# Retention and SwiGLU on one core: norms, token sums and weight sums dealt out as single operations, attention begun in a group's last unit

## The chip, the cores and the metric

The kernel runs on one NeuronCore of a Trainium2 chip. Five engines work beside each other, each with a queue of instructions that it takes strictly in order: TensorE (PE in the profile; its weight loads are PEld), VectorE (DVE), ScalarE (ACT), GpSimd (POOL) and SyncE (SP), which issues DMA transfers. An instruction that waits for a semaphore holds up everything behind it in its own queue. The metric is the device time of one execution in microseconds, here the median of repeated runs.

## The reference

Four sequences of 768 tokens with eight heads of 64 columns go through retention (a linear attention with decay, in blocks), and the result, 3072 tokens by 512 columns, through a gated MLP with 1536 hidden columns.

```python
for b in range(nb):                                  # blocks of a sequence
    intra = np.einsum('bhic,bhjc->bhij', qb, kb) * Dmask[None]
    intra = np.einsum('bhij,bhjd->bhid', intra, vb)
    inter = np.einsum('bhid,bhde->bhie', qb * lam_pow[None], kv_state)
    out[:, :, sl] = intra + inter
    kv_state = lam_block * kv_state + np.einsum('bhsd,bhse->bhde', kb_dec, vb)
...
xn = x / np.sqrt(np.mean(x * x, axis=-1, keepdims=True) + 1e-6) * rms_g
g, val = xn @ w_gate, xn @ w_val
out = (g / (1 + np.exp(-g)) * val) @ w_out
```

## The kernel before, in words

The 3072 tokens are six groups `m` of 512, and the hidden columns are twelve slices `f` of 128. A unit is one slice for one group: gate and value products, SiLU times value, and the product with 128 rows of `w_out`, which adds to four PSUM accumulators. To keep single-precision accuracy each operand is split into a high and a low half-precision part, and a product takes three passes (high by high, low by high, high by low).

The units run in this order (variable `u`): 0 to 5 are slices 0 to 5 of group 0, in a written-out opening that also loads and splits the weights; 6 to 17 are group 1; 18 to 23 are slices 6 to 11 of group 0; 24 to 35 are group 2, and 36 to 47, 48 to 59 and 60 to 71 are groups 3, 4 and 5. Up to unit 23 a unit (`unit`) has 24 gate and value matmuls 512 wide. From unit 24 on (`unit_of_sums`) a unit takes seven products of half that size instead of eight, a Winograd-like scheme over the two halves of the gate and value weights and of the token columns. It needs sums of weight blocks (`weight_sums`) and sums of token blocks (`Norm.sums`), each again split into a high and a low part.

Three kinds of work run beside the units:

- **Attention.** A group has four head pairs (`Pair`). A pair takes two units: in the first (`new`) scores (L479), decays of k (ACT, L489), of the scores (DVE, L495) and of q (POOL, L499), and in the second (`done`) state sums, states (DVE, L523), the mix (L539, L550), the copy of the output (ACT, L571), its squares (ACT, L582) and their sum (L588). In groups 2 to 4 the pairs of the next group stand in units 0 to 7: `new` in even units, `done` in odd ones.
- **The norm of the next group** (`Norm`) stands in units 8 to 11 of a group: squares split (step 8), their column sums on TensorE, a seed (L658, L662), three Newton steps of three DVE operations each (`refine`, L669 to L671; one in step 8, two in step 9), then `parts(0)` in step 10 and `parts(1)` in step 11: two scalings (L679), four sums (L695 to L698), casts to the high parts (ACT, L684, L701) and the low parts (L687, L705). For group 2 this stands in units 21 to 23.
- **Weights.** `halve_o` turns a slice of `w_out` into half-precision parts (ACT, ACT, DVE, POOL: L263, L264, L265, L268), two slices in each of units 18 to 23. `weight_sums(f)` does for slice f two POOL additions that make whole weights (`r`, L805), four DVE sums (`ws`, L808 to L811), three ACT casts (L815 to L817) and three POOL subtractions (L818 to L820). It is issued whole at the end of units 18 to 23 (slices 0 to 5) and 26 to 31 (slices 6 to 11).

The order is that of the code: `tc.manual_schedule` keeps every engine's instructions in the order in which the Python code issues them. In a product unit the DVE order that matters is: `sum` into `val` (left), the low part of the unit before (`hh`, L940), attention's decay or states, `sum` into `sg` (right), `sum` into `val` (right), then `mul_sums` (L909). On ACT: `keep` (L897), the high part of the unit before (L933), two more `keep`, then `silu_half(1)`, `silu_half(0)` (L904). TensorE's product banks are one double tile (`pp`) in one unit and two single tiles (`pa`, `pb`) in the next; before, `pp` is that of odd `u`.

In units up to 23 the DVE multiplication that ends a unit is L922, in later units L909; both are used below as the tick of a unit.

## Time and profile before

| | us |
|---|---|
| median of 3 runs (767.11 to 783.88) | 767.44 |
| the profiled execution's own time | 771.88 |
| its span, first to last instruction | 769.9 |
| TensorE busy | 675.0 |
| VectorE busy | 420.5 |
| ScalarE busy | 329.9 |
| GpSimd busy | 161.0 |
| mean granted TensorE clock | 0.949 of full |

A row of a group view gives engine, line of the kernel, operation, tiles as out<-in, their shapes, and how often; a timeline row begins with start and duration in us; a row of the chain of waits gives start, duration and what the end of the run depended on then. A row of a stretch gives its bounds, its length, each engine's busy time with the instructions in brackets, the granted clock, the DMA share and GB/s.

### The profile page before, as it was taken

The page shows a single profiled execution, that of the slowest core. Times are in us where ns is not written, and L with a number is a line of the kernel's source. Part 1 is how long each engine was busy: PE and PEld are TensorE (multiplying, and loading weights), DVE is VectorE, ACT ScalarE, POOL GpSimd, SP SyncE. Part 2 cuts the span into 40 slices and gives each one's busy share as a digit, 9 for nine tenths or more (in the row PEclk, how much of TensorE's full clock was granted, in tenths as well). Part 3 has the DMA queues.
Part 4 walks back from the last instruction along what each step waited for, and adds up shares of the span by engine and source line. Part 5 has one row for each costly group of instructions (what it writes and reads, how often), then busy time and mean ns, then how long its engine had stood idle before and what let it go on. Part 6 is the DMA issues. An engine that isn't in the chain of part 4 may idle for free.

```text
span 769.9 us, 12275 instructions
## 1 busy us (share of the span) xinstructions
PE 675.0 (88%) x5007; PEld 450.4 (58%) x5007; DVE 420.5 (55%) x793; ACT 329.9 (43%) x674; POOL 161.0 (21%) x150
## 2 busy tenths in 40 slices
PE   9999999999987718887977799997899997799997
PEld 8656655556543305655645577765577765566664
DVE  7898667874446754435464543365444456443333
ACT  4786457762354342433333343333343433343332
POOL 3101200111367343354422101102101101100000
PEclk9999999999988957989999999998899999899999
DMA  8966224311300001111100031110031000010001
GB/s 326 331 229 209 110 85 162 137 55 35 131 1 1 0 1 55 55 55 55 55 2 1 1 110 56 55 56 1 0 111 55 2 1 1 0 55 1 1 1 55
DMA packets 14311, 51.12 MB, mean 66 GB/s; under 512 B 1712, under 2 KB 1968, under 8 KB 12848
## 3 DMA queue, kind: packets, MB, share of 16 engines
q1 hardware_dynamic: 13968, 49.69, 18.2%
q8 instruction: 39, 0.64, 0.3%
q10 hardware_dynamic: 288, 0.66, 0.3%
q14 instruction: 16, 0.13, 0.1%
HBM read 44.05 MB, written 6.29 MB: 65 GB/s over the span
## 4 chain that ended last, share of the span: by engine, by line
PE 69%; DVE 16%; ACT 8%; POOL 4%; issue 2%; DMA 1%; DVEq 0%; SPq 0%; ACTq 0%; POOLq 0%
PE pp L854 13%; PE pa L854 8%; PE acc L741 7%; PE pg L722 6%; PE pv L722 6%; PE acc L743 6%; PE acc L742 6%; PE pb L854 6%; PE pa L479 3%; PE po L539 3%; POOL r L805 2%; PE po L550 2%; DVE xn L679 1%; DVE sg L909 1%; DVE yt L670 1%
## 5 line engine op out<-in xcount | busy, mean ns | idle before, releaser
L742 PE MATMUL acc<-wo,hh 128*128 128x512 f16 (+1 forms) x288 | 113.3, 393 | 0.0
L743 PE MATMUL acc<-wo,hh 128*128 128x512 f16 (+1 forms) x288 | 113.1, 393 | 0.0
L854 PEld LDWEIGHTS <-wo 128*128 128x128 f16 x576 | 57.7, 103 | 66.3 <-issue 44.7
L741 PE MATMUL acc<-wo,hh 128*128 128x512 f16 x216 | 85.6, 396 | 0.2 <-DVE hh L940 0.2
L854 PEld LDWEIGHTS <-wg 128*128 128x128 f16 x576 | 56.4, 98 | 47.4 <-issue 26.5
L854 PEld LDWEIGHTS <-wv 128*128 128x128 f16 x576 | 58.0, 101 | 28.3 <-issue 19.7
L722 PE MATMUL pg<-x,wg 128*128 128x512 f16 x288 | 67.8, 380 | 3.3 <-ACT sg L915 3.0
L897 ACT COPY tx<-pp 128x256 f32<-128x256 f32 x72 | 26.7, 371 | 102.5 <-PE pp L854 102.5
L722 PE MATMUL pv<-x,wv 128*128 128x512 f16 x288 | 66.8, 379 | 0.0
L897 ACT COPY tx<-pa 128x256 f32<-128x256 f32 x72 | 26.8, 372 | 87.9 <-PE pa L854 87.6
L933 ACT CAST hh<-sg 128x512 f16<-128x512 f32 (+1 forms) x72 | 44.5, 618 | 39.4 <-DVE sg L922 19.3
L854 PE MATMUL pp<-tx,wo 128*128 128x256 f16 x288 | 42.5, 287 | 21.5 <-DVE vals L900 21.5
L854 PE MATMUL pp<-x,wg 128*128 128x256 f16 x288 | 40.5, 278 | 22.6 <-ACT sg L904 17.8
L900 DVE TENSOR_TENSOR vals<-pp,tx 128x256 f32<-128x256 f32 x48 | 20.3, 424 | 61.2 <-PE pp L854 50.1
L499 POOL TENSOR_TENSOR qkv<-qkv,pw 128x512 f32<-128x512 f32 x22 | 28.5, 1298 | 113.9 <-PE pa L479 108.4
L722 PEld LDWEIGHTS <-wg 128*128 128x128 f16 x288 | 26.4, 98 | 36.8 <-issue 7.8
L940 DVE TENSOR_TENSOR hh<-sg,hh 128x512 f16<-128x512 f32 x54 | 41.5, 768 | 11.1 <-ACT hh L933 8.7
L722 PEld LDWEIGHTS <-wv 128*128 128x128 f16 x288 | 27.6, 98 | 33.3 <-issue 1.1
L900 DVE TENSOR_TENSOR vals<-pb,tx 128x256 f32<-128x256 f32 x48 | 20.3, 424 | 46.7 <-PE pb L854 38.4
L909 DVE SCALAR_TENSOR_TENSOR sg<-vals,cv,sg 128x512 f32<-128x512 f32 x48 | 39.0, 812 | 9.0 <-ACT sg L904 5.9
L854 PE MATMUL pa<-x,wv 128*128 128x256 f16 x144 | 21.8, 290 | 19.1 <-ACT sg L915 9.9
L743 PEld LDWEIGHTS <-hh 128*128 128x128 f16 x216 | 21.8, 101 | 27.7 <-issue 3.8
(179 smaller groups left out, 1255.7 us busy)
## 6 DMA issues: line engine op xcount, KB each, us to landing
qkv<-in_qkv_dram SPq DMA_DIRECT2D x47, 512.0 KB, 5.1
raw_gv<-in_weights_dram SPq DMA_DIRECT2D x11, 1024.0 KB, 6.0
raw_o<-in_weights_dram SPq DMA_DIRECT2D x12, 512.0 KB, 4.0
out_dram<-o SPq DMA_DIRECT2D x23, 256.0 KB, 2.1
partial<-in_weights_dram SPq DMA_DIRECT2D x2, 512.0 KB, 11.6
qkv<-in_qkv_dram ACTq DMA_DIRECT2D x1, 512.0 KB, 4.3
out_dram<-o SPq DMA_DIRECT2D x1, 128.0 KB, 2.1
out_dram<-o ACTq DMA_DIRECT2D x1, 128.0 KB, 1.9
```

The lines of the kernel that those rows point to most:

```text
L479: nc.tensor.matmul(self.pa[:, j, c, :], self.kT[r, c, :], self.qT[r, c, :], start=True, stop=True,)
L499: eng.tensor_mul(self.qT, self.qT, pw[:, p : p + 1, :].broadcast_to([P, GC, P]))
L722: nc.tensor.matmul(ps, w[:, kk, :], x[:, kk, :], start=i == kk == 0, stop=i == 2 and kk == NK - 1,)
L741: nc.tensor.matmul(acc, hl[:, ts_], oh, start=first, stop=False)
L742: nc.tensor.matmul(acc, hh[:, ts_], ol, start=False, stop=False)
L743: nc.tensor.matmul(acc, hh[:, ts_], oh, start=False, stop=last)
L854: nc.tensor.matmul(ps, w(ow, k), x(ox, k), start=first and i == k == 0, stop=i == 2 and k == 1, skip_group_check=True,)
L897: nc.scalar.copy(self.kept[:, i], self.pa)
L900: nc.vector.tensor_add(out, self.pb, self.kept[:, i])
L909: nc.vector.scalar_tensor_tensor(self.sg, self.val, cv[:, self.f : self.f + 1], self.sg, ALU.mult, ALU.mult)
L933: nc.scalar.copy(self.hh, self.sg)
L940: nc.vector.tensor_sub(self.hl, self.sg, hh)
```

## The change

1. `weight_sums` becomes a class with four steps. `whole` (POOL) is issued at the end of the unit before, `sums` (DVE) within the unit, `high` (ACT) and `low` (POOL) after it. The slices go to units 18, 19, 20 and then 24 to 32, one each. `halve_o` goes to units 18, 19, 20 with three slices each, and to 24, 25, 26 with one each; units 21 to 23 keep only the norm.
2. The norm's operations in units 8 to 11 become a list of single tasks with assumed costs; after `add(5)` and before `add(4)` each unit takes from it what fits a given room (1.4 to 2.9). The ACT casts have a list of their own. Row sums and seed stand in step 7 instead of 8; what is left when the group ends is issued then.
3. Attention of the next group begins one unit earlier: the first pair's `new` stands in unit 11 of the group before (in unit 23 for group 3), so `new` has odd and `done` even units. The banks swap with it: `pp` is now that of even `u`.
4. `val` and `kept` are one buffer each instead of two that alternate; scaled tokens take the tiles of the seed.

```diff
-    def weight_sums(f, rest):
...
+    class WeightSums:
...
+        def whole(self, u):
...
+            for i, w in enumerate((wv, wg)):
+                nc.gpsimd.tensor_add(self.r[:, i], w[:, f, 0], w[:, f, 1])
...
+        def high(self):
+            for to, t in self.places():
+                nc.scalar.copy(to[:, 0], t)
...
+        def low(self, eng=nc.gpsimd):
+            for to, t in self.places():
+                eng.tensor_sub(to[:, 1], t, to[:, 0])
...
-            self.val = vals[u % 2]
-            self.kept = copies[u % 2]
+            self.kept = spare[0]
+            self.val = spare[1].rearrange("p a g -> p (a g)")
...
-    HALVE = {18: [6, 7], 19: [8, 9], 20: [10, 11], 21: [0, 1], 22: [2, 3], 23: [4, 5]}
+    HALVE = {18: [6, 7, 8], 19: [9, 10, 11], 20: [0, 1, 2], 24: [3], 25: [4], 26: [5]}
+    SUMS = {u: WeightSums(f) for f, u in enumerate([18, 19, 20, *range(24, 33)])}
...
+        def run(self, room):
+            while self.todo and self.todo[0][0] <= room + 0.05:
+                cost, fn, args = self.todo.pop(0)
+                room -= cost
+                fn(*args)
...
+        casts.run(1.5)
         h.add(5, b, True)
...
-        if norm and step == 9:
-            norm.refine()
-            norm.refine()
+        if u in SUMS:
+            SUMS[u].sums(u)
+        tasks.run(1.6 if attention or u in SUMS else 2.9)
         h.add(7, a)
         h.keep(0)
         h.sum(h.sg[:, right], 0)
         h.silu_half(1, h.sg[:, right])
+        if u in SUMS:
+            SUMS[u].high()
+            SUMS[u].low()
...
-        if norm and step == 10:
-            norm.parts(0, (nc.gpsimd, nc.gpsimd, nc.gpsimd))
-        if norm and step == 11:
-            norm.parts(1, (nc.vector, nc.vector, nc.gpsimd))
+        for i in HALVE.get(u, []):
+            halve_o(i)
+        if norm:
+            norm.row_sums()
+            norm.seed()
+        else:
+            tasks.run(1.4)
         h.add(4, a)
...
+            if u == 2 * NF - 1:
+                new = Pair(3, 0)
...
+            following = m + 2 if f == NF - 1 else m + 1
+            if f % 2 and p < NP and following < NG:
+                new = Pair(following, p)
+            if f % 2 == 0:
+                done = pair
```

Where it moves instructions, at three places that the prediction uses.

**DVE, units 8 and 9 of group 3** (tiles: `hy`, `yt` the norm of group 4, `pss` its sums, `pb_3_8` and `pp_3_9` the product banks, `sg` the SiLU input). Before:

```order
L900 TENSOR_TENSOR sg_3_8_4541<-pb_3_8_4540,tx_0_2466 128x256
L658 TENSOR_SCALAR hy_4_4599<-pss_4_4596 128x512
L662 TENSOR_SCALAR hy_4_4599<-hy_4_4599 128x512
L669 TENSOR_TENSOR yt_4_4600<-hy_4_4599 128x512
L670 TENSOR_TENSOR yt_4_4600<-yt_4_4600,hy_4_4599 128x512
L671 SCALAR_TENSOR_TENSOR hy_4_4599<-yt_4_4600,hy_4_4599 128x512
L900 TENSOR_TENSOR vals_2638<-pb_3_8_4540,tx_0_2466 128x256
L909 SCALAR_TENSOR_TENSOR sg_3_8_4541<-vals_2638,cv_138,sg_3_8_4541 128x512
```

Now, in unit 8:

```order
L976 TENSOR_TENSOR hh_3_7_4557<-sg_3_7_4465,hh_3_7_4557 128x512
L671 TENSOR_TENSOR yt_4_4524<-hy_4_4523 128x512
L673 TENSOR_TENSOR yt_4_4524<-yt_4_4524,hy_4_4523 128x512
L675 SCALAR_TENSOR_TENSOR hy_4_4523<-yt_4_4524,hy_4_4523 128x512
L671 TENSOR_TENSOR yt_4_4524<-hy_4_4523 128x512
L936 TENSOR_TENSOR sg_3_8_4543<-pp_3_8_4542,tx_0_2458 128x256
L673 TENSOR_TENSOR yt_4_4524<-yt_4_4524,hy_4_4523 128x512
L675 SCALAR_TENSOR_TENSOR hy_4_4523<-yt_4_4524,hy_4_4523 128x512
L936 TENSOR_TENSOR tx_1_2459<-pp_3_8_4542,tx_0_2458 128x256
```

Five operations of the norm stood in one block behind the SiLU's sum; now four stand ahead of it and two behind.

**POOL, units 18 and 19** (group 0, slices 6 and 7; `rest` and `wo16` of the halvings, `r` the whole weights, `ws` the weight sums, `sq_2` the squares of attention, `qkv` its q). Before:

```order
L268 TENSOR_TENSOR wo16_6_2093<-rest_6_2094 128x512
L268 TENSOR_TENSOR wo16_7_2099<-rest_7_2100 128x512
L588 TENSOR_TENSOR sq_2_1994<-sq_2_1994,sq_2_1_2123 128x512
L805 TENSOR_TENSOR r_0_2153<-wv_131 128x512
L805 TENSOR_TENSOR r_0_2153<-wg_130 128x512
L818 TENSOR_TENSOR wo16_6_2093<-ws_0_2156,wo16_6_2093 128x512
L819 TENSOR_TENSOR col_133<-ws_0_2156,col_133 128x256
L820 TENSOR_TENSOR wg_130<-ws_0_2156,wg_130 128x256
```

Now, in the same units:

```order
L268 TENSOR_TENSOR wo16_6_2101<-rest_6_2102 128x512
L268 TENSOR_TENSOR wo16_7_2107<-rest_7_2108 128x512
L268 TENSOR_TENSOR wo16_8_2113<-rest_8_2114 128x512
L857 TENSOR_TENSOR wo16_6_2101<-ws_0_2028,wo16_6_2101 128x512
L857 TENSOR_TENSOR col_133<-ws_0_2028,col_133 128x256
L857 TENSOR_TENSOR wg_130<-ws_0_2028,wg_130 128x256
L588 TENSOR_TENSOR sq_2_1994<-sq_2_1994,sq_2_1_2143 128x512
L829 TENSOR_TENSOR r_1_2173<-wv_131 128x512
L829 TENSOR_TENSOR r_1_2173<-wg_130 128x512
```

The subtractions of slice 0 now stand ahead of the squares, the whole weights behind them are those of the next slice (`r_1`), and three halvings instead of two stand in front.

**ACT, a unit of group 2 with `done` attention and weight sums** (before unit 27, now unit 26; `sg` the two SiLU halves, `x_3` and `sq_3` the output of attention and its squares). Before:

```order
L904 ACTIVATE sg_2_3_2924<-sg_2_3_2924,cg_136 128x256
L571 COPY x_3_2800<-po_3_1_2961 128x512
L904 ACTIVATE sg_2_3_2924<-pp_2_3_2923,cg_136 128x256
L582 ACTIVATE sq_3_1_3012<-po_3_1_2961 128x512
L815 CAST wo16_1_2418<-ws_7_3029 128x512
L816 CAST partial_96<-ws_7_3029 128x256
L817 CAST wg_130<-ws_7_3029 128x256
```

Now:

```order
L940 ACTIVATE sg_2_2_2816<-sg_2_2_2816,cg_136 128x256
L852 CAST wo16_11_2249<-ws_5_2873 128x512
L852 CAST col_133<-ws_5_2873 128x256
L852 CAST wg_130<-ws_5_2873 128x256
L571 COPY x_3_2681<-po_3_1_2850 128x512
L263 ACTIVATE wo16_5_2904<-wo_5_1046,ts_132 128x512
L264 ACTIVATE rest_5_2905<-wo_5_1046,ts_132 128x512
L940 ACTIVATE sg_2_2_2816<-pp_2_2_2815,cg_136 128x256
L582 ACTIVATE sq_3_1_2925<-po_3_1_2850 128x512
```

The three casts, and in units 24 to 26 two operations of a halving, now stand between the two SiLU halves instead of behind both.

More of the change, by code (lines that the diff above doesn't have):

```diff
@@ L1356, in unit @@
         elif norm:
-            norm.parts(step - NP - 2, (nc.vector, nc.vector, nc.gpsimd))
+            norm.parts(step - NP - 2)
         if before:
@@ L1392, in out @@
                 outs.out(*ts)
+        attention = new or done
         h.banks(u)
@@ L1407, in unit_of_sums @@
             new.decay_q()
-        elif done:
+        elif done and not begun:
             done.state_sums()
-        if not new:
+        else:
             out(0)
-        if norm and step == 8:
+        if norm:
             norm.split_squares()
```

198 lines of the change are left out of this document (125 added, 73 removed).

## The prediction

> **What bounds the kernel now.** The page first, then stretches of it, then the ticks of the units.
>
> ```profile
> span 769.9 us, 12275 instructions
> PE 675.0 (88%) x5007; PEld 450.4 (58%) x5007; DVE 420.5 (55%) x793; ACT 329.9 (43%) x674; POOL 161.0 (21%) x150
> ```
>
> TensorE is busy 88% of the span, so about 95 us can be won from its waits, and more if its busy time shrinks. Up to unit 18, at 191 us, the order is the same but for POOL's first whole weights, so I begin with the stretch behind them (bounds, length, busy time of PE, PEld, DVE, ACT, POOL; granted clock):
>
> ```profile
> 191.73:303.80 112.07, 76.77 (x451) 41.97 (x450) 61.40 (x104) 42.08 (x78) 55.53 (x50) 0.82 0.09 33
> ```
>
> Units 18 to 23 and the start of group 2 leave TensorE idle for 35 of 112 us, at a clock of 0.82. The ticks L909 (DVE, start and duration) measure the groups from there on:
>
> ```profile
> 303.77 0.75 DVE L909 SCALAR_TENSOR_TENSOR sg<-vals,cv,sg 128x512 f32<-128x512 f32 x1
> 320.80 0.75 DVE L909 SCALAR_TENSOR_TENSOR sg<-vals,cv,sg 128x512 f32<-128x512 f32 x1
> 384.57 0.75 DVE L909 SCALAR_TENSOR_TENSOR sg<-vals,cv,sg 128x512 f32<-128x512 f32 x1
> ...
> 440.78 0.75 DVE L909 SCALAR_TENSOR_TENSOR sg<-vals,cv,sg 128x512 f32<-128x512 f32 x1
> 558.69 0.75 DVE L909 SCALAR_TENSOR_TENSOR sg<-vals,cv,sg 128x512 f32<-128x512 f32 x1
> 577.22 0.75 DVE L909 SCALAR_TENSOR_TENSOR sg<-vals,cv,sg 128x512 f32<-128x512 f32 x1
> 675.11 0.75 DVE L909 SCALAR_TENSOR_TENSOR sg<-vals,cv,sg 128x512 f32<-128x512 f32 x1
> 683.44 0.75 DVE L909 SCALAR_TENSOR_TENSOR sg<-vals,cv,sg 128x512 f32<-128x512 f32 x1
> 690.61 0.75 DVE L909 SCALAR_TENSOR_TENSOR sg<-vals,cv,sg 128x512 f32<-128x512 f32 x1
> ```
>
> These are unit 0 of group 2, its units 2 and 7, unit 0 of groups 3 and 4, unit 2 of group 4, and units 0, 1, 2 of group 5. From unit 0 to unit 0, group 2 takes 137.0, group 3 117.9, group 4 116.4. Two plain units take 15.5 (8.33 and 7.17, the double bank `pp` being the slower), two units with a pair of attention 18.5 (558.69 to 577.22). Four pairs and four plain units would be 4 x 18.5 + 2 x 15.5 = 105. So 12 us a group are the norm's, and 20 more in group 2 the weight sums': its units 3 to 7 take 12.75 each (320.80 to 384.57).
>
> What such a stall is made of, for the weight sums of unit 18 and the start of the next units, in the chain of waits (start, duration, what):
>
> ```profile
> 202.54 0.71 ACT rest L264
> 203.25 0.47 ACT x L571
> ...
> 204.21 0.97 ACT o L748 x2
> ...
> 205.85 2.79 DMA out_dram<-o
> ...
> 208.77 2.27 POOL r L805 x2
> 211.06 0.43 DVE ws L808
> ...
> 212.31 0.47 ACT wo L815
> ...
> 213.54 0.81 ACT qkv L489 x2
> ...
> 214.96 0.75 DVE sg L922
> ...
> 218.26 0.67 DVE rest L265
> ...
> 228.88 0.76 DVE sg L922
> ...
> 231.01 0.70 DVE rest L265
> ```
>
> An output transfer frees a buffer, POOL makes the whole weights, DVE sums, ACT casts, and only behind the casts comes the next unit's SiLU, then its tick (L922) at 214.96. The halvings follow, then POOL again: one ring through four engines. And the norm, in units 8 to 11 of group 3:
>
> ```profile
> 511.09 0.70 DVE hy L658
> ...
> 512.27 0.70 DVE yt L669
> ...
> 529.23 1.32 DVE xn L679 x2
> ...
> 532.05 1.14 ACT x L684 x2
> 533.19 0.73 ACT tx L701
> ...
> 535.95 1.44 PE pp L854 x6
> ```
>
> Seed, Newton steps, scalings, sums and casts stand in the chain themselves, while TensorE waits; it comes back at 535.95 with 1.44 us for six matmuls.
>
> **Part 1: units 18 to 23.** More rows of its steps: the tick of unit 18, a unit's value product, the first product of unit 24 that isn't held, and POOL's operations.
>
> ```profile
> 197.41 0.75 DVE L922 SCALAR_TENSOR_TENSOR sg<-pv,cv,sg 128x512 f32<-128x512 f32 x1 [0.87 <-PE pv L722]
> ```
>
> ```profile
> 172.43 2.59 PE pv L722 x12
> ```
>
> ```profile
> 287.06 1.22 PE L854 MATMUL pa<-x,wv 128*128 128x256 f16 x5 [9.18 <-ACT x L684]
> ```
>
> ```profile
> 213.01 1.15 POOL L818 TENSOR_TENSOR wo<-ws,wo 128x512 f16<-128x512 f32 x1 [1.98 <-ACT wo L815]
> 215.38 1.27 POOL L499 TENSOR_TENSOR qkv<-qkv,pw 128x512 f32<-128x512 f32 x1
> ...
> 280.52 1.26 POOL L268 TENSOR_TENSOR wo<-rest 128x512 f16<-128x512 f32 x1 [1.77 <-DVE rest L265]
> 282.71 1.64 POOL L268 TENSOR_TENSOR wo<-rest 128x512 f16<-128x512 f32 x1 [0.93 <-DVE rest L265]
> ```
>
> Before: 197.41 to 287.06, 89.7. A slice's subtractions take 2.4 (213.01 to 215.38), its whole weights 2.3, its sums 1.7 (1.25 to 212.31, and a fourth), its casts 1.2 (to 213.54), a halving's addition 1.3. The tiles `ws` and `rest` share two buffers; since `ws` now lives through the halvings, these run on one, as at 280.52 and 282.71: 2.2 apart.
>
> - Unit 18, from its tick: first halving on DVE +3.5 (it was 3.3 from 214.96 to 218.26), the third 4.4 later, its copy on ACT 0.7: +8.6. Casts 1.2, output and squares 1.0, two output copies 1.0: +11.8. The buffer is free 3.6 later (205.18 to 208.77), whole weights and sums with their gaps 4.2: **19.6**. It was 17.6 (197.41 to 214.96).
> - Unit 19: the third halving's addition ends at +9.8 (3.3 + 4.4 + 0.8 + 1.3), then subtractions 2.4, squares 1.3, whole weights 2.3, sums 1.8: **17.6**.
> - Unit 20, without attention's decay and states: the halvings start at +2.1 (228.88 to 231.01); copy, casts, output and squares end at +9.4. Only then is the value bank free for unit 21, whose twelve matmuls take 2.6, or 5.2 at the half pace that follows a wait. TensorE has waited; I take 4.3: **13.7**.
> - Unit 21, norm alone: 2.1, seed 1.2, nine operations of 0.7: **9.6**. Unit 22: 2.1, scalings 1.3, sums 1.5, casts 1.9, decay of k 0.8, SiLU 0.6: **8.2**. Unit 23, to the first cast: 3.5 + 1.3 + 1.5 + 0.6, and a fourth state 0.2: **7.1**.
>
> Sum 75.8, a gain of 13.9: the first three units are no quicker than before, the three that have given up halvings and sums are. Unit 24 takes 16.7 from its first product to its tick (303.77). Now its sums wait for POOL (subtraction of token sums, then 2.3), ready at about +5; they stand in DVE's queue ahead of the SiLU's sum, and casts, attention's output and a halving (1.2 + 0.5 + 1.4) ahead of the second SiLU half: I get 14.0, 2.7 less. **Together 16.6.**
>
> **Part 2: group 2.** Its bare time is four pairs and four plain units, 105 by the ticks, plus row sums 0.5 and about 0.4 where the norm's tasks exceed the gap of a `pp` unit. Eight weight-sum units (25 to 32) come on top. Their waits: DVE's sums wait for POOL's whole weights, and behind them in DVE's queue are the SiLU's sum and the tick. On ACT:
>
> ```profile
> 328.94 0.51 ACT L904 ACTIVATE sg<-sg,cg 128x256 f32<-128x256 f32 x1 [0.49 <-DVE sg L900]
> 330.23 0.47 ACT L904 ACTIVATE sg<-pp,cg 128x256 f32<-128x256 f32 x1 [0.32 <-PE pp L854]
> ```
>
> The second half starts 1.3 after the first. With casts and output between it starts 0.5 + 1.2 + 0.5 = 2.2 after (late by 0.9), with a halving 3.6 (late by 2.3). In a `pp` unit TensorE waits for that: units 26, 28, 30 pay 2.3 + 0.9 + 0.9; unit 25 pays 1.6 at its tick, unit 32, where norm tasks join, 2.2. In single-bank units the bank isn't needed soon, so 27, 29, 31 pay nothing there. Sum 7.9 (25 and 32 by the same count from their own order). POOL's new place also slows DVE:
>
> ```profile
> L909 DVE SCALAR_TENSOR_TENSOR sg<-vals,cv,sg x48: 750/752/1481, 303.8 to 761.0; 128x512 f32<-128x512 f32 x48
> ```
>
> 0.75 usually, 1.48 at most. I put 0.3 on each of nine units, 2.7: half the 0.73 on every second unit would be 1.6, 0.73 on each 6.6; the tick has a unit of slack before its result is used, so I stay near the low end. [...]
>
> The group's end: what is left of the second `parts` stands behind the last tick, so tick 0.75, sums 1.5, a cast 0.6 and a low part 0.7 (the size of a Newton operation) lie ahead of the next group's first product, 3.6 in all, and 0.8 for slow matmuls (six at 1.44): 4.4. Group 2: 105 + 0.9 + 7.9 + 2.7 + 4.4 = 120.9 against 137.0, **a gain of 16.1.**
>
> **Part 3: groups 3 and 4.** For norm 4 the order puts the sums ahead of the last tick, leaving cast and low part: 2.4. Group 3: 105 + 0.9 + 2.4 = 108.3, **9.6 less**. For norm 5 only one low part is late, 1.0; group 4 now has three pairs and six plain units (its first pair moved into group 3): 55.5 + 46.5 + 0.9 + 1.0 = 103.9, **12.5 less**. Every group's first pair moves with all its DMAs: SP's loads are issued a unit sooner, their order among the outputs is kept, and a pair's load is several units ahead of its use; that costs nothing. Left out of hiding, one such unit would lose at most the 1 us by which a pair's first unit exceeds a plain one.
>
> **Part 4: the rest.** Group 5 has eleven intervals; with the banks swapped six are the short kind instead of five: 8.33 - 7.17 = **1.2 less**. One buffer for `val` and `kept`: DVE's next `val` already follows the tick in its queue, and `kept` is read on DVE before ACT writes it again; between 0 and 0.1 a unit, taken as 0.
>
> **Sum:** 16.6 + 16.1 + 9.6 + 12.5 + 1.2 = 56.0. The profiled execution, 771.88 with a span of 769.9, would become 715.9. The median of the runs is 767.44, 4.4 below it; the same 56.0 off the median gives **711.4**.
>
> **Rivals.**
> - *The weight sums don't fit a unit.* The ring POOL, DVE, ACT, POOL stays closed over each unit, at the 12.75 of units 3 to 7 of group 2. For: those very operations ran at that pace. Against: ring and unit are now out of step by one unit. My units 25 to 32 take 55.5 + 15.5 + 0.5 + 7.9 + 2.4 = 81.8; at 12.75 they take 102: 20 more, **732**. Operations held beside POOL (1.48 for 0.75) are one way into it. 0.15.
> - *Everything is hidden:* weight-sum units cost nothing beyond bare ones, 7.9 + 2.7 less: **701**. For: POOL and ACT have idle time in every unit. Against: ACT's order above. 0.15.
> - *The norm's tasks still count:* in-order DVE hands each one's length on to the SiLU, so groups 3 and 4 keep their time: 9.6 + 12.5 more, **734**. Against: a gap of some 2 us ahead of each SiLU sum in plain units. 0.07.
> - *Slower:* unit 18's ring in my own sum, 19.6, holds in all nine weight-sum units, because whole weights wait behind squares, these behind the second SiLU half, and that behind the casts. Mine take 14.0 + 81.8 + 0.3 = 96.1; 9 x 19.6 is 176, 80 more: **792**. From 96.1 + 56.0 + 15.3 = 167.4, or 18.6 a unit, on, the whole is over 2% slower. Against: no halving stands in six of them, and no output buffer is waited for. 0.03.
>
> The order shows the norm's operations apart and the sums in their units, so that the change does not do what it says is excluded.
>
> **Chances.** My case has 0.57, from 704 to 722 by its own unknowns (DVE's slowing 1.6 to 6.6, group ends from half to double, units 18 to 23 by 3). The first and third rival together, 754, have 0.03. The range 700 to 734 ends at the neighbours on each side, of which about half lies outside, so it holds some 0.8. A measurement of this kernel tells about 2% from no change, 752 and 783: faster by more 0.94 (my case and the first three rivals), within 0.03 (both together), slower 0.03.
>
> **What would show it.** Ticks of units 18 to 23 about 19.6, 17.6, 13.7, 9.6, 8.2 apart: right in part 1; under 14 for unit 18 says the buffer chain is not there. Group 2 from unit 0 to unit 0 near 121, groups 3 and 4 near 108 and 104; in units 24 and 26 the second SiLU half begins right behind the halving. I am wrong if weight-sum units reach 12.75, or if TensorE waits for DVE in units 8 to 10.

## The result and the profile after

The changed kernel takes 724.04 us (median of 4, 722.93 to 725.24), the kernel before 768.9 beside it: a ratio of 0.941, 95% interval 0.937 to 0.945. One execution of the kernel before (783.88) and one of casts_late below (793.90) ran over 2% slower than the others of their kernel and are not counted in the ratios. The profiled execution is the one of 722.93. Its page, the first lines:

```profile
span 721.1 us, 12347 instructions
PE 662.8 (92%) x5007; PEld 444.3 (62%) x5007; DVE 423.2 (59%) x799; ACT 329.1 (46%) x674; POOL 158.4 (22%) x144
```

TensorE's busy time is 12 us shorter with the same 5007 matmuls, and its idle time fell from 95 to 58. The same stretch as before, then groups 2, 3, 4 and the eleven intervals of group 5, each from tick to tick (bounds, length, busy time of PE, PEld, DVE, ACT, POOL; granted clock):

```profile
191.73:303.80 112.07, 91.72 (x623) 52.55 (x621) 64.55 (x123) 45.61 (x87) 52.28 (x45) 0.91 0.13 44
286.13:409.96 123.83, 106.78 (x876) 75.23 (x874) 77.50 (x141) 53.64 (x123) 60.26 (x52) 0.96 0.14 45
409.96:520.89 110.93, 103.62 (x880) 74.42 (x879) 58.35 (x106) 44.16 (x97) 13.25 (x9) 1.00 0.14 48
520.89:627.15 106.26, 99.90 (x832) 72.16 (x831) 56.38 (x103) 42.36 (x93) 11.14 (x8) 1.00 0.06 23
627.15:712.24 85.09, 80.64 (x593) 57.78 (x592) 31.22 (x58) 30.68 (x68) 0.00 (x0) 1.00 0.04 13
```

The first row has the same bounds in time as before, but more work lies between them (623 matmuls in place of 451): TensorE's idle time there has fallen from 35 to 20 us. The granted clock rose in all but group 5, which had 1.00 before (first row 0.82 to 0.91, group 2 0.93 to 0.96, groups 3 and 4 to 1.00). The same two columns of before for groups 3 and 4:

```profile
440.78:558.69 117.91, 107.31 (x876) 76.17 (x875) 56.44 (x104) 44.49 (x97) 15.02 (x11) 0.96 0.14 46
558.69:675.11 116.42, 105.47 (x876) 75.03 (x875) 55.81 (x104) 43.58 (x95) 13.75 (x10) 0.97 0.08 28
```

In group 3 TensorE idled 10.6 and now 7.3; the other 3.7 of the gain is nearly the same matmuls (880 and 876) at a higher granted clock. Group 4 also has 44 matmuls fewer: what its first pair had behind the tick of unit 0 now lies ahead of it.

What each stretch gained, measured from tick to tick in the two profiled executions:

| stretch | before | predicted | after | gain predicted | gain |
|---|---|---|---|---|---|
| tick of unit 18 to tick of unit 24 | 106.4 | 89.8 | 88.6 | 16.6 | 17.8 |
| group 2 | 137.0 | 120.9 | 123.8 | 16.1 | 13.2 |
| group 3 | 117.9 | 108.3 | 110.9 | 9.6 | 7.0 |
| group 4 | 116.4 | 103.9 | 106.3 | 12.5 | 10.2 |
| group 5 | 85.9 | 84.7 | 85.1 | 1.2 | 0.8 |

Unrounded, the sum is 48.8 where 56.0 was predicted; the two profiled executions' own times differ by 48.95. Within group 2, the eight units 25 to 32 take 83.6 (predicted 81.8). What sets them, in the chain of waits, from unit 26 to unit 28 (start, duration, what):

```profile
304.66 0.52 ACT wo L852
...
306.37 0.67 POOL col L857
...
309.38 1.79 POOL sq L588
311.18 2.69 POOL r L829 x2
...
313.89 1.47 DVE ws L840
...
316.61 0.35 DVE sg L936
...
316.98 0.51 ACT sg L940
317.49 0.52 ACT wo L852
...
327.80 0.39 ACT sg L940
328.23 0.83 PE pp L890 x6
```

Casts, low parts and the added squares on POOL, POOL's whole weights, DVE's sums, and only behind these the SiLU's sum (316.61), the SiLU and the next casts: the ring POOL, DVE, ACT, POOL still closes once a unit. The prediction had this only as a rival. The last two rows are the prediction's own term: in unit 28 TensorE waits for the second SiLU half, which stands on ACT behind the casts and attention's output. TensorE's waits for the SiLU's steps in the eight units (in all, times, longest):

```profile
PE pp L890 <- ACT sg L940: 3.2, 4, 1.2
PE pp L890 <- DVE sg L936: 2.6, 1, 2.6
PE pb L890 <- DVE sg L936: 1.3, 2, 0.8
PE pst L508 <- ACT sg L940: 1.1, 1, 1.1
```

That is 4.3 for the second half on ACT, in just the units in which the prediction had it (25, 26, 28, 30 and 32: 1.1, 1.2, 0.4, 0.4 and 1.2, where it had 1.6, 2.3, 0.9, 0.9 and 2.2), and 3.9 for the SiLU's sum on DVE, for which it had nothing. Another 3.0 are for the value's sum; the same eight units of group 3, without weight sums, have 1.8 of these.

### The profile page after: what moved, and what is told of

Its sections match the earlier page's. It is cut to its first block, busy times and chain, and to the rows that moved or that the text cites. A ratio compares the mean times of both kernels' runs of the same rounds, so it can differ in the third digit from the quotient of the medians.

```text
span 721.1 us, 12347 instructions
## 1 busy us (share of the span) xinstructions
PE 662.8 (92%) x5007; PEld 444.3 (62%) x5007; DVE 423.2 (59%) x799; ACT 329.1 (46%) x674; POOL 158.4 (22%) x144
## 4 chain that ended last, share of the span: by engine, by line
PE 44%; DVE 9%; ACT 6%; POOL 3%; issue 2%; DVEq 0%; ACTq 0%
PE pp L890 14%; PE pa L890 7%; PE pb L890 5%; PE acc L758 5%; PE acc L759 4%; PE acc L760 4%; DVE tx L936 2%; ACT sg L940 2%; PE po L539 2%; POOL r L829 1%; DVE sg L945 1%; ACT tx L933 1%; PE pa L479 1%; PE po L550 1%; DVE ws L840 1%
## 5 line engine op out<-in xcount | busy, mean ns | idle before, releaser
L759 PE MATMUL acc<-wo,hh 128*128 128x512 f16 (+1 forms) x288 | 111.4, 387 | 0.0
L760 PE MATMUL acc<-wo,hh 128*128 128x512 f16 (+1 forms) x288 | 111.3, 386 | 0.0
L758 PE MATMUL acc<-wo,hh 128*128 128x512 f16 x216 | 83.3, 386 | 0.2 <-DVE hh L976 0.2
L890 PEld LDWEIGHTS <-wo 128*128 128x128 f16 x576 | 55.8, 98 | 38.3 <-issue 16.5
L499 POOL TENSOR_TENSOR qkv<-qkv,pw 128x512 f32<-128x512 f32 x22 | 29.2, 1330 | 127.7 <-PE pa L479 122.6
L936 DVE TENSOR_TENSOR tx<-pp,tx 128x256 f32<-128x256 f32 x48 | 20.4, 424 | 62.7 <-PE pp L890 51.0
L890 PE MATMUL pp<-x,wg 128*128 128x256 f16 x288 | 39.8, 275 | 15.5 <-ACT sg L940 12.9
L890 PE MATMUL pp<-tx,wo 128*128 128x256 f16 x288 | 40.0, 275 | 11.6 <-DVE tx L936 11.6
L890 PE MATMUL pp<-x,wv 128*128 128x256 f16 x288 | 37.5, 278 | 9.5 <-ACT x L688 6.9
L976 DVE TENSOR_TENSOR hh<-sg,hh 128x512 f16<-128x512 f32 x54 | 39.5, 731 | 9.3 <-ACT hh L969 7.7
L945 DVE SCALAR_TENSOR_TENSOR sg<-tx,cv,sg 128x512 f32<-128x512 f32 x48 | 39.1, 815 | 5.2 <-ACT sg L940 2.2
L940 ACT ACTIVATE sg<-sg,cg 128x256 f32<-128x256 f32 x48 | 24.4, 509 | 36.8 <-DVE sg L936 36.8
L936 DVE TENSOR_TENSOR tx<-pb,tx 128x256 f32<-128x256 f32 x48 | 20.4, 424 | 32.3 <-PE pb L890 29.5
```

The costliest lines, as they stand in the source:

```text
L499: eng.tensor_mul(self.qT, self.qT, pw[:, p : p + 1, :].broadcast_to([P, GC, P]))
L758: nc.tensor.matmul(acc, hl[:, ts_], oh, start=first, stop=False)
L759: nc.tensor.matmul(acc, hh[:, ts_], ol, start=False, stop=False)
L760: nc.tensor.matmul(acc, hh[:, ts_], oh, start=False, stop=last)
L890: nc.tensor.matmul(ps, w(ow, k), x(ox, k), start=first and i == k == 0, stop=i == 2 and k == 1, skip_group_check=True,)
L936: nc.vector.tensor_add(out, self.pb, self.kept[:, i])
```

## The experiments

Theory at the outset: the norm's single operations fit the gaps, the weight sums nearly so, and what they still cost is ACT, late for the second SiLU half. Rivals: fewer waits for another reason (a plain unit more for the norm), and the ring through POOL as what is left. Each run stands beside runs of the kernel before on its chip (medians 771.4 to 772.4), and ratios are against those (the first row's against the runs of the section above). "Eight units" is from the tick of unit 24 to that of unit 32; the columns are read from the ticks of each profiled execution, a single one for each kernel.

| kernel | us | ratio to before (95%) | eight units | group 2 | group 3 | group 4 |
|---|---|---|---|---|---|---|
| after | 724.0 | 0.941 (0.937-0.945) | 83.6 | 123.8 | 110.9 | 106.3 |
| norm_in_blocks | 746.5 | 0.968 (0.965-0.971) | 85.4 | 130.3 | 117.4 | 116.3 |
| sums_in_blocks | 751.8 | 0.975 (0.972-0.978) | 107.7 | 146.6 | 111.1 | 106.3 |
| whole_early | 723.6 | 0.938 (0.935-0.940) | 82.6 | 121.8 | 112.0 | 106.3 |
| out0_early | 719.9 | 0.934 (0.931-0.936) | 82.4 | 122.6 | 108.8 | 104.7 |
| attention_late | 732.5 | 0.952 (0.947-0.957) | 82.3 | 122.5 | 113.6 | 114.2 |
| casts_late | 728.2 | 0.946 (0.938-0.954) | 89.0 | 128.1 | 113.4 | 106.3 |
| sums_behind | 718.7 | 0.934 (0.929-0.939) | 79.2 | 117.7 | 113.1 | 106.2 |
| behind_early_out0 | 708.1 | 0.921 (0.916-0.926) | 75.2 | 113.5 | 108.7 | 104.7 |
| fuller_gaps | 706.2 | 0.915 (0.914-0.917) | 76.3 | 111.3 | 107.3 | 106.8 |
| low_sums_on_dve | 707.4 | 0.916 (0.914-0.918) | 75.2 | 113.9 | 107.3 | 105.0 |
| two_halvings | 704.0 | 0.913 (0.911-0.915) | 78.5 | 118.2 | 110.0 | 104.7 |
| all_together | 701.7 | 0.909 (0.907-0.910) | 78.5 | 118.0 | 106.3 | 104.4 |

**Undo the norm's part.** (norm_in_blocks)

```diff
-        tasks.run(1.6 if attention or u in SUMS else 2.9)
+        if block and f == 9:
+            block.refine()
+            block.refine()
...
             norm.seed()
-        else:
-            tasks.run(1.4)
+            norm.refine()
+        if block and f == 10:
+            block.parts(0)
+        if block and f == 11:
+            block.parts(1)
```

> The changed kernel, with the norm of groups 3, 4 and 5 (prepared in groups 2, 3 and 4) put back into blocks: seed and one Newton step in unit 7, two steps in unit 9, a whole `parts` in unit 10 and one in unit 11. Nothing else differs. My account: the gaps ahead of the SiLU's sum hold single operations and not blocks, so the norm's 12 us a group come back, less the tails that the dealt-out norm has at the group ends now; by the prediction's terms 12 - 4.8 in group 2, 12 - 3.3 in group 3, 12 - 1.9 in group 4, 26 in all: 750, with group 3 from unit 0 to unit 0 near 120 where it is 110.9 now. Rival (what helps is that a group has one plain unit more for the norm, and not the dealing out): groups keep 111 and 106 within 2, under 730.

746.5: 22.5 come back (6.5, 6.5 and 10.0 in groups 2, 3 and 4), and the rival falls. Dealing out the norm is about half of the whole gain.

**Undo the weight sums' part** (of the units from 24 on). (sums_in_blocks)

```diff
-        if u in SUMS:
-            SUMS[u].sums(u)
...
-            SUMS[u].high()
-            SUMS[u].low()
...
         h.mul_sums()
         if u + 1 in SUMS:
             SUMS[u + 1].whole(u)
+            SUMS[u + 1].sums(u + 1)
+            SUMS[u + 1].high()
+            SUMS[u + 1].low()
```

> The changed kernel, with the weight sums of units 24 to 32 put back into one block at the end of the unit ahead (whole weights on POOL, sums on DVE, casts on ACT, low parts on POOL, one right behind the other); units 18 to 23 and the norm stay dealt out. My account: the ring POOL, DVE, ACT, POOL then stands ahead of the next unit's SiLU again, at the 12.75 us of before: units 25 to 32 take about 102 where they take 83.6, the time about 742. Rival (the ring through POOL sets the pace in either order, since the chain of the changed kernel still runs through POOL's whole weights and DVE's sums in these units): 84 to 88 for the eight units, 724 to 729.

751.8, and 107.7 for the eight units, 13.5 each: worse than the expected 12.75. Two lines from its chain of waits, six and sixteen matmuls right behind such a block:

```profile
311.86 1.44 PE pp L890 x6
313.30 1.91 PE po L539 x16
```

1.44 and 1.91, where the changed kernel has 0.82 and 1.02 (at 512.04 and 512.86 of its chain): in this run TensorE's matmuls right behind such a block take longer too. The granted clock of the whole profiled execution is 0.963 where the changed kernel's is 0.981, and the latter is below 1.00 in two of these eight units, at 0.87. Ring and unit being out of step does matter; the ring's pace is not the same in either order.

**Open the ring through POOL.** (whole_early)

```diff
         if u in SUMS:
             SUMS[u].sums(u)
+            if u + 1 in SUMS:
+                SUMS[u + 1].whole(u)
...
         h.mul_sums()
-        if u + 1 in SUMS:
-            SUMS[u + 1].whole(u)
```

> The changed kernel, with one move in units 24 to 31: POOL adds the next unit's whole weights right behind this unit's sums, ahead of this unit's low parts and of the added squares, and not behind them at the unit's end. The ring through POOL is so opened and nothing is taken away. The prediction put the loss of units 25 to 32 on ACT, whose casts stand between the two SiLU halves (7.9 us); by that the move brings nothing: 722 to 725, the eight units 83 to 84. Rival, from the changed kernel's chain of waits (eight pairs of POOL's whole weights with 2.69 us each stand right ahead of DVE's sums, and DVE's SiLU sum behind those): the wait for POOL goes, the eight units fall by 4 to 9, to 75 to 80, and the time to 715 to 720.

723.6, the eight units 82.6: as good as nothing, as the prediction's account has it. But the timeline shows something beside ACT. In unit 28 DVE's sums no longer wait for POOL, they run beside it:

```profile
322.97 1.15 POOL L829 TENSOR_TENSOR r<-wv 128x512 f32<-128x512 f16 x1 [1.52 <-PE po L539]
324.08 1.33 POOL L829 TENSOR_TENSOR r<-wg 128x512 f32<-128x512 f16 x1
```

```profile
322.99 1.41 DVE L840 TENSOR_TENSOR ws<-r 128x256 f32<-128x256 f32 x1
324.33 1.37 DVE L841 TENSOR_TENSOR ws<-r 128x256 f32<-128x256 f32 x1
325.73 0.42 DVE L842 TENSOR_TENSOR ws<-r,ws 128x256 f32<-128x256 f32 x1
```

Two of the four sums take 1.4 in place of 0.42, each ending just behind an operation of POOL (324.12 and 325.41). Here the wait has turned into a longer operation, still ahead of the SiLU's sum. It is so in three of the eight units (28, 30 and 31: seven of their twelve sums, 6.6 us longer in all; in the changed kernel three sums, 3.2). In the other five the sums take their 0.42, so this is a part of why the move brings little, and not shown to be all of it.

**Move ACT's casts.** (casts_late)

```diff
-        if u in SUMS:
-            SUMS[u].high()
-            SUMS[u].low()
...
         h.silu_half(0, a)
+        if u in SUMS:
+            SUMS[u].high()
+            SUMS[u].low()
```

> The changed kernel, with one move in units 24 to 32: ACT's casts of the weight sums (1.2) and POOL's low parts stand behind the second SiLU half and not between the two halves. The prediction's term of 7.9 (ACT late for the second half) has about 5 of its parts in these casts, the rest in halvings: by it units 24 to 32 fall by 4 to 6, 718 to 720. Rival (a ring sets these units, through POOL or, as with the whole weights moved forward, through DVE: the low parts then come later by as much as the SiLU comes sooner): the eight units stay at 82 to 86, the time at 722 to 727.

728.2, the eight units 89.0 instead of 78 to 80: with the casts gone from between the halves they are 5.4 longer, not shorter. TensorE's waits for the same steps in the eight units (in all, times, longest):

```profile
PE pb L890 <- DVE sg L936: 7.2, 4, 3.0
PE pp L890 <- DVE sg L936: 4.2, 3, 2.6
PE pp L890 <- ACT sg L940: 1.1, 2, 0.6
```

The wait for the second half on ACT falls from 4.3 to 1.1, so the casts between the halves did cause such a wait; but the wait for the SiLU's sum on DVE grows from 3.9 to 11.4. Low parts, and with them the next whole weights and sums, come later by what the casts were moved, and the ring binds. That the casts alone set these units' time falls; what they would cost with the ring open was not tried. (Group 3, whose code is the same, took 2.4 longer in the profiled execution; see the last section.)

**Take the sums out of the SiLU's way.** (sums_behind, behind_early_out0)

```diff
-        if u in SUMS:
-            SUMS[u].sums(u)
...
         h.silu_half(1, h.sg[:, right])
-        if u in SUMS:
-            SUMS[u].high()
-            SUMS[u].low()
+        if u in SUMS:
+            SUMS[u].sums(u)
...
         h.silu_half(0, a)
+        if u in SUMS:
+            SUMS[u].high()
+            SUMS[u].low()
```

> The changed kernel, with DVE's four sums of the weight sums (1.7) placed behind the SiLU's sum in units 24 to 32, their casts and low parts behind the second SiLU half; POOL's whole weights stay at the unit's end. So nothing of the weight sums stands ahead of the SiLU any more, on DVE or on ACT. My theory now (what lengthened the eight units is DVE's order: its sums wait, for POOL or for their share of the memory beside POOL, and the SiLU's sum waits behind them): 83.6 falls to 72 to 77, the time to 713 to 718. Rival (POOL's ring of whole weights, sums, casts and low parts has a length of its own, some 9 to 10, that binds wherever the sums stand): 81 to 88, 721 to 728.

79.2 for the eight units, between the two: 4.4 won, by sums and casts together, since the casts move with the sums. The share of the memory, one of the two things for which the theory lets DVE's sums wait, no run shows; what the runs show is operations of DVE that end just behind one of POOL (last section). Some of the ring is still there, so the next kernel adds both other moves (the edit of the whole weights as above, and that of the first output tile below).

> As the kernel with the sums behind the SiLU's sum, and in addition whole weights right behind the sums (ring through POOL opened) and the first output tile of units that end a pair ahead of product 6 (worth 4.2 by itself). If order on DVE is the whole of it, this is 4 to 5 below the kernel with the sums behind alone: 708 to 713. If the ring through POOL binds there and not here, it is lower by 10 and more. If POOL's operations beside DVE's are the price, the eight units stay over 78 and the time over 714.

708.1 and 75.2. Against the early output tile alone (82.4) the two moves together give 7.2, where each alone gave 4.4 and 1.0. That fits two rings of about one length, one through POOL's queue and one through DVE's own order, where opening one leaves the other; their lengths were not measured apart. The whole is 10.5 below sums_behind where 4 to 5 were expected, but only 4.0 of that lie in the eight units; 4.4 lie in group 3, half of them from the output tile and the rest from its last interval, in which sums_behind has six matmuls at 1.44 in place of 0.82 (last section). Bare, by groups 3 and 4 of the same kernel, the eight units would be 3 x 18.2 + 16.1 = 70.7; 4.5 stay.

**The first output tile.** (out0_early)

```diff
         elif done and not begun:
             done.state_sums()
-        else:
+        if not new:
             out(0)
...
             done.mix_chunks()
-            if not begun:
-                out(0)
```

> The changed kernel, with the first output tile's three matmuls (0.75 us) of a unit that ends a pair of attention put back ahead of product 6, where the kernel before has them, and not behind the chunks' mixing. The prediction carried over 18.5 us for two units with a pair; the changed kernel takes 8.4 + 10.3 to 10.6. My account: TensorE now waits about 0.45 there for the value's sum on DVE, since only the state sums (0.5) cover it: such units fall to 10.0, 11 of them by 0.3 to 0.5, 4 in all: 720. Rival (the 0.3 comes from the single buffer of `val` and `kept`, or is taken by the next wait on the way): they stay at 10.3 and more, 723 to 725.

719.9. In the changed kernel, in a unit that ends a pair, TensorE has only the state sums between the first twelve products and product 6:

```profile
436.33 1.47 PE L890 MATMUL pp<-x,wv 128*128 128x256 f16 x12
437.73 0.57 PE L508 MATMUL pst<-qkv 128*64 128x64 f32 x12
438.77 0.81 PE L890 MATMUL pp<-tx,wo 128*128 128x256 f16 x6 [0.47 <-DVE tx L936]
```

In out0_early, in the chain of waits:

```profile
419.57 0.50 PE pst L508 x12
420.07 0.32 PE acc L758
...
420.82 0.66 PE pp L890 x6
```

The wait of 0.47 for the value's sum is gone, such units take 9.8 and 10.0 instead of 10.35 and 10.57 (0.53 each), and two units with a pair 18.2. Group 3 falls to 108.8 and group 4 to 104.7, near the 108.3 and 103.9 of the prediction.

**Attention begins where it began.** (attention_late)

```diff
-            if f % 2 and p < NP and following < NG:
-                new = Pair(following, p)
-            if f % 2 == 0:
+            p = f // 2
+            if f % 2 == 0 and p < NP and m + 1 < NG:
+                new = Pair(m + 1, p)
+            if f % 2:
                 done = pair
-            if m + 1 < NG and f == 2 * NP - 1:
+            if m + 1 < NG and f == 2 * NP:
```

The pair begun in unit 23 goes with it, and `banks` has the double bank in odd units again.

> The changed kernel, with attention put back: a pair begins in units 0, 2, 4, 6 of its own group and ends in 1, 3, 5, 7, none begins in the last unit of the group ahead, the double bank `pp` is in odd units again, and the norm starts in unit 8 in place of 7. Weight sums and the norm's single operations stay. The prediction took the move of the pairs as free and the swapped banks as 1.2: by it 725 to 727. Rival: the move is what gives the norm's operations a fourth unit; without it three units hold at most 3 x (2.9 + 1.4) = 12.9 of their 14.2, less what doesn't fit, and the rest stands at the group's end: 2 to 4 more in each of three groups, 731 to 738.

732.5: the move is worth 8.5, not nothing. Its places: group 4 is 7.9 longer (its last interval 13.8 in place of 9.0, where what is left of the norm stands; the other 3.1 are mostly the pair that the change had moved ahead of it), group 3 2.7, group 5 1.4; group 2 and units 18 to 23 are 3.5 shorter together. The last intervals of groups 2, 3 and 4 alone are 6.4 longer. That the norm gets a fourth unit is so a real part of the change, which the prediction had only in the order's rows of the group ends.

**The group ends and the halvings**, from the kernel of 708.1 on.

```diff
-        tasks.run(1.6 if attention or u in SUMS else 2.9)
+        tasks.run(1.6 if attention or u in SUMS else 3.6)
...
-        else:
-            tasks.run(1.4)
         h.add(4, a)
         h.silu_half(0, a)
+        if not norm:
+            tasks.run(2.1)
```

> The kernel with the weight sums behind the SiLU's sum and the early first output tile (708.1), with two edits for the norm: rooms of 3.6 and 2.1 us in place of 2.9 and 1.4, and the second run of single operations behind the second SiLU half in the order (so ACT's casts no longer stand between the halves). Then nothing of the norm is left behind a group's last tick in groups 3 and 4. The prediction's group-end terms (4.4, 2.4, 1.0) say that what stands there is paid in full: the last intervals of groups 2 and 3 go from 14.8 and 13.0 to 10 to 11, units with the casts from 9.5 to 8.4, the time to 699 to 703. Rival (the gaps are no longer than the 2.9 and 1.4, and what is taken from the end is paid in units 8 to 11, with DVE late for the SiLU's sum): these units longer by 0.5 to 1 each, 705 to 709.

706.2. The last intervals of groups 2 and 3 fall to 9.8 and 10.0 as expected, 8 less in all; but units 8 to 11 grow by 2.8, 1.6 and 2.7 in groups 2, 3 and 4, and the end of group 4 had only 0.6 to win. TensorE's largest wait in units 10 and 11 of group 3 (in all, times, longest):

```profile
PE pp L890 <- DVE sg L936: 1.8, 1, 1.8
```

DVE is late for the SiLU's sum there: the gaps hold about the 2.9 and 1.4, and not 3.6 and 2.1.

```diff
-            tasks.add(0.1, rest, norm.low_sums, i, 1)
+            tasks.add(0.1, rest, lambda i: norm.low_sums(i, nc.vector), i, 1)
```

> The kernel with the weight sums behind the SiLU's sum and the early first output tile (708.1), with the low parts of the token sums (768 wide) on DVE instead of POOL, in the same place of the order. In the changed kernel a low part of x on DVE at the end of group 3 took 2.13 in place of 0.69, beside POOL's 1.90 for these low parts, and TensorE's first product waits for it. If DVE is held by POOL there, the last intervals of groups 2 and 3 (14.8 and 13.0) fall by about 1.4 each, though DVE has about 1.0 more to do behind: 705 to 706. Rival (the long duration has another cause, or DVE's added 1.0 stands on the path): the intervals stay or grow by 1, 708 to 710.

707.4, not the 705 to 706 expected: 1.4 less at the end of group 3, but 0.4 more at that of group 2, where POOL's low parts had come behind DVE's, and 0.4 more in group 4. DVE's low parts of x (L691, duration min, median and max in ns), with the sums' low parts on POOL (behind_early_out0) and on DVE (low_sums_on_dve):

```profile
L691 DVE TENSOR_TENSOR x<-xn,x x8: 681/683/2128, 32.3 to 602.7; 128x512 f16<-128x512 f32 x8
```

```profile
L691 DVE TENSOR_TENSOR x<-xn,x x8: 681/684/687, 32.4 to 602.0; 128x512 f16<-128x512 f32 x8
```

The 2.13 is gone with POOL's neighbour, so that was its cause.

```diff
-    HALVE = {18: [6, 7, 8], 19: [9, 10, 11], 20: [0, 1, 2], 24: [3], 25: [4], 26: [5]}
+    HALVE = {18: [6, 7], 19: [8, 9], 20: [10, 11], 24: [0], 25: [1], 26: [2], 27: [3], 28: [4], 29: [5]}
```

> The kernel with the weight sums behind the SiLU's sum and the early first output tile (708.1), with two halvings in place of three in units 18 to 20, and the six that remain one by one in units 24 to 29 (where 24 to 26 had one each). By part 1 of the prediction halvings stand in the rings of units 18 to 20, 2.2 apart: units 18, 19 and 20 fall from 20.2, 17.2 and 12.2 to 13.8 by 2.2 each, 6.6 in all, and units 27 to 29 get 0 to 1.4 each: 703 to 705. Rival (the ring of output buffer, whole weights and sums sets units 18 and 19, halvings or not): 20.2 and 17.2 stay, 708 to 711.

704.0. Units 18, 19 and 20 take 17.7, 15.0 and 10.0 where they took 20.2, 17.2 and 13.8: 2.5, 2.2 and 3.8 less. The eight units give 3.3 back. Halvings do stand in the rings of those units, at the 2.2 that the prediction gave them. Of the 3.8 of unit 20, 1.6 are DVE's wait for the value product: 3.55 without this edit, 1.90 with it, and 1.91 in the changed kernel's profiled execution, whose unit 20 took 12.2.

And all of it together, with the second run of tasks behind the second SiLU half as in the first of these diffs, but with the rooms 2.9 and 1.4:

> The edits that helped, together: sums behind the SiLU's sum, whole weights behind the sums, the early first output tile, two halvings a unit in 18 to 20, the low parts of the token sums on DVE; and the second run of the norm's operations behind the second SiLU half, with the rooms of before (2.9 and 1.4). If the gains add up: 708.1 - 4.2 (halvings) - 0.8 (low parts) - 1.1 in each of groups 3 and 4 (their 9.5 units, where ACT's three casts stand between the halves) = 701. Rival (DVE's low part behind the casts is now the later one, and the tick waits for it): these units stay at 9.5 or grow to 10, 703 to 705.

701.7, as added up; the 9.5 units are at 8.55. This kernel beats both: 0.909 of the time before (0.907 to 0.910), 22 us under the changed one.

## Why the prediction was right, and where it was off

A cut of 7.3% was forecast and one of 5.9% came. The time lies in the range of 700 to 734 and 12.6 above the figure; it is 2 above the 704 to 722 that I gave to my own case, in the part that the range keeps for its neighbours.

- **Part 1** held step by step. POOL's whole weights in unit 18 do wait for an output transfer,

  ```profile
  212.81 1.15 POOL L829 TENSOR_TENSOR r<-wv 128x512 f32<-128x512 f16 x1 [1.09 <-DMA out_dram<-o]
  ```

  and those of unit 19 follow the squares on POOL. The ticks of units 18 to 23 are 20.2, 17.2, 12.2, 9.7, 8.2 apart and 7.0 to unit 24's first product (forecast 19.6, 17.6, 13.7, 9.6, 8.2, 7.1); unit 24 took 14.0 from there, as worked out. For unit 20 I took 4.3 for the value product, between 2.6 and 5.2; it was 2.75 in the profiled execution of after; 4.25, and 13.7 for the unit, came in that of out0_early. So most of the 1.2 by which the stretch beat the forecast of 89.8 is luck of one execution: norm_in_blocks, with the same code up to unit 24 and 13.8 for unit 20, takes 89.4. The halvings' removal showed their 2.2.
- **Part 2, ACT late for the second half, 7.9: sum right, but by two errors.** What the eight units cost over bare ones is 83.6 - (3 x 18.73 + 7.7 + 8.5) = 11.2, against 10.3 forecast. The term itself is there, in the units named, at about half its size: 4.3. What the prediction put at nothing is the wait for the SiLU's sum on DVE, 3.9, behind POOL's whole weights and DVE's sums. Moving the casts alone lengthened the units; moving DVE's sums and POOL's whole weights, with the casts, won 7.2. By these runs the first rival's ring, at 10.4 a unit instead of 12.75, closed through POOL's queue and through DVE's, binds first. The step that failed is the reading of ACT's order as the only cause, and that the sum came so near is luck. Behind it, the count of DVE slowed by POOL (2.7) was right that it happens and can't be told from the ring by its size.
- **Parts 2 and 3, two units with a pair at 18.5: carried over from before, though the change moves the first output tile of such units** from ahead of product 6 to behind the chunks' mixing. I had not followed that line of the diff. It costs 0.53 in each of 11 units: out0_early takes 2.1 off group 3 and 1.6 off group 4, most of their shortfall of 2.6 and 2.4.
- **Part 3, the norm in the gaps:** right; its undoing costs 22.5. That moving the pairs costs nothing was right, that it earns nothing was implied and wrong: 8.5, most of it by the fourth unit for the norm. The group ends, forecast at 4.4 and 2.4, were worth 5.0 and 3.0 in fuller_gaps. What Part 2 counted for the weight sums' casts, Part 3 left out for the norm's: three casts between the SiLU halves make one unit of groups 3 and 4 9.5 long in place of 8.4, with TensorE waiting 1.7 for ACT there, and 8.55 with them moved behind. There ACT's order is the cause.
- **Part 4, 1.2:** 0.8; units with the double bank take 8.39 instead of 8.33, perhaps the single buffer, which wasn't tried by itself.
- **The base.** The sum was made against the profiled 771.88 and then set off the median of three, 767.44. Later medians of the same kernel are 771.4 to 772.4: by these the profiled execution was the typical one, and 715.9 the better forecast. That is 4.4 of the 12.6; 7.1 are the sum, 1.1 the distance of after's profiled execution from its median.
- **The rivals:** the pace of 12.75 is what the blocks have (13.5), so dealing out is what avoided it; that everything is hidden is not so even at 708.1, where 4.5 stay; the norm that still counts is excluded; a ring of 19.6 in all nine units did not come. Of the signs of being wrong, one weight-sum unit reached 12.75 (unit 25 to 26, 12.9, at a clock of 0.87), and in units 8 to 10 of group 3 TensorE waits 0.7 for DVE and 2.3 for ACT.

## What to carry to other kernels

A ring through several in-order queues may open only when each queue that closes it is rearranged: here one edit alone brought 1.0, the other 4.4, and both together 7.2. The chain of waits names only the wait that ended last, so read the engine's list of waits beside it: here the list has two causes of about one size. A sum that comes out can hide two errors, so check its terms one by one. When a unit's duration is carried over from the trace of before, go through the diff for every instruction that leaves or enters that unit, also the ones that look like tidying. Put independent work where the queue has just released the critical operation, not ahead of it; weight sums and casts behind the SiLU won 4.4 in eight units.

## What the runs showed of the hardware

**POOL holds DVE.** Beside the rows of whole_early above, the low part of x at the end of group 3 in the timeline of the changed kernel:

```profile
508.31 1.90 POOL L721 TENSOR_TENSOR tx<-xt,tx 128x768 f16<-128x768 f32 x1 [3.90 <-ACT tx L717]
508.62 2.13 DVE L691 TENSOR_TENSOR x<-xn,x 128x512 f16<-128x512 f32 x1
```

It takes 2.13 in place of 0.69 and ends 0.54 behind POOL's operation, counted as busy all the while. In the profile of before, the two ticks of 1.48 in place of 0.75 (at 332.71 and 359.35), the longest of the 48 in the prediction's row, run beside POOL's whole weights. The first of them:

```profile
332.49 1.15 POOL L805 TENSOR_TENSOR r<-wv 128x512 f32<-128x512 f16 x1
333.61 1.59 POOL L805 TENSOR_TENSOR r<-wg 128x512 f32<-128x512 f16 x1
```

```profile
332.71 1.48 DVE L909 SCALAR_TENSOR_TENSOR sg<-vals,cv,sg 128x512 f32<-128x512 f32 x1
```

Not every operation of DVE beside POOL is held: attention's decay (L495), which takes one input from PSUM, never lengthened, though an operation of POOL, mostly its multiplication of q (L499), runs beside it in 18 of 24 cases. Two rows of the timeline, and L495's line with min, median and max of its durations:

```profile
430.67 1.34 POOL L499 TENSOR_TENSOR qkv<-qkv,pw 128x512 f32<-128x512 f32 x1 [2.16 <-PE pa L479]
430.79 1.22 DVE L495 TENSOR_TENSOR a<-pa,mask 128x1024 f32<-128x1024 f32 x1
```

```profile
L495 DVE TENSOR_TENSOR a<-pa,mask x24: 1210/1218/1225, 6.5 to 560.9; 128x1024 f32<-128x1024 f32 x24
```

Why the ones are held and L495 is not, no run shows. In the changed kernel's timeline, from unit 18 on, 17 operations of DVE are longer than usual by more than 0.15, each beside an operation of POOL, by 11 us together; whether TensorE waits for each of them was not measured.

**A wait sometimes costs twice.** The end of group 3, with the same code and the same wait, in after and in casts_late (chain of waits; six matmuls of product 6):

```profile
508.10 2.66 DVE x L691 x2
...
512.04 0.82 PE pp L890 x6
```

```profile
510.94 2.66 DVE x L691 x2
...
514.98 1.44 PE pp L890 x6
```

Both have 2.66 of DVE's low parts ahead of the first product; behind it six matmuls take 0.82 in the one and 1.44 in the other, and the interval 13.5 and 16.0. The granted clock (the number behind POOL's) tells them apart, in the stretches of after and of casts_late:

```profile
507.35:520.89 13.54, 10.70 (x103) 7.50 (x101) 6.12 (x10) 4.46 (x10) 1.90 (x1) 1.00 0.20 60
512.00:526.00 14.00, 12.63 (x97) 8.37 (x96) 4.17 (x8) 3.57 (x8) 1.03 (x1) 0.76 0.17 51
```

In unit 20 both executions have a slow stretch, but at different places. The gate and the value product in after, then in out0_early:

```profile
238.67 3.54 PE L739 MATMUL pg<-x,wg 128*128 128x512 f16 x12
244.29 2.75 PE L739 MATMUL pv<-x,wv 128*128 128x512 f16 x12 [2.08 <-ACT sq L582]
```

```profile
237.94 2.76 PE L739 MATMUL pg<-x,wg 128*128 128x512 f16 x12
244.42 4.25 PE L739 MATMUL pv<-x,wv 128*128 128x512 f16 x12 [3.71 <-ACT sq L582]
```

In after it falls on the gate product ahead of the wait for ACT, which is only shorter by it, 2.08 in place of 3.71; in out0_early on the value product behind the wait, and the interval is 13.7 in place of 12.2. From unit 18 on, TensorE stands idle for 2 us or more ahead of a matmul 16 times in the profile of before and 7 times in that of after; in the 3 us from the start of that matmul the granted clock is 0.50, for all or a part of them, in 15 and in 5 of these cases. What decides it no run shows; the runs show that the same wait comes out both ways. For the comparison of single profiled executions it means that the end of group 3, behind such a wait, is known to within 2.4 only.
